# Attention and a gated layer on one core: all sums of GpSimd given to VectorE, and one order for all instructions drawn up anew

## The chip, the cores and the metric

The kernel runs on 1 core of one Trainium2 chip. The metric is device time in microseconds (us), the median of several runs; lower is better. The engines are TensorE (PE in the profile; its weight loads PEld), VectorE (DVE), ScalarE (ACT), GpSimd (POOL) and SyncE (SP), whose queue issues all transfers of this kernel.

## The reference

For each of 8 batches and 8 heads there are 512 tokens `x` (64 wide) and 32 states. Tokens attend to states and states to tokens; the two results, laid side by side as 8 x 544 rows of 512, go through a layer with a product of two branches.

```
a  = softmax(scale * x @ state.T);  xread = a @ state
a2 = softmax(scale * state @ x.T);  sread = a2 @ x
rows = concatenate([xread, sread], axis=2)      # 8*544 rows of 512
out  = ((rows @ w_a) * (rows @ w_b)) @ w_out    # 512 -> 1536 -> 512
```

## The kernel before

**The arithmetic.** Every large product is made of three matmuls, since each float32 operand is held as a high part (`_h`) and a remainder (`_l`): high by high, high by remainder, remainder by high. A high part is made by a ScalarE copy that rounds, its remainder by a VectorE subtraction: `g_h` and `g_l` of the gated value, `p_h` and `p_l` of the first weights, `at_h` and `at_l` of the attention, `ws_h` and `ws_l` of sums of weights. The weights of the first layer are folded with the states (`products`, or `project` by way of the DRAM tensors `scr`, read back as `p_raw`).

**The stages.** The 1536 inner columns are 12 tiles, two to a chunk `c` (0 to 5). `VISITS` walks the batches 0 to 3 over their chunks: `layer1` fills two PSUM tiles `ab` per inner tile, ScalarE copies the one into `a_sb`, VectorE multiplies the other with it, and `layer2` accumulates four `acc` tiles. Batches 4 to 7 come in pairs (`ROUNDS`, two rounds a pair): `make` lets `layer1` keep its product of 512 columns in `kept_g`, and seven calls of `term` multiply sums of the two batches' values with sums of the weights, seven block products in place of eight. Beside the rounds stand `attend` (attention of batches 4 to 7), `reading` (the states' side; it loads `a` from `e_dram` and `xn`) and the states' own layer (`states1`, `states2`, tiles `sw_st`).

**The sums that GpSimd makes.** They all go through `pool_op` (L1106). `combine(c)` (L1109) makes the sums of weights of a chunk: 2 of 512 columns into `wf` (high part and remainder joined), 4 of 256 columns into `ws`, and 2 remainders of 512 columns into `ws_l`, 8 in all; their results go to DRAM as `s_dram` and come back as `wt`. `term` (L1192) with k = 3 makes 4 sums of 512 columns: `kept_g` less `kept_g`, `t2w`, `kept_g` less `t2w`, and `kept_g` less `kept_g`. There are 6 chunks with 8 and 12 terms with 4, so 96 sums: 72 of 512 columns and 24 of 256.

**The order.** The program is first recorded, not issued: `Recorder` keeps each instruction (or a group that stays together) as a numbered unit in the order of the source. `ORDER` is a table of all unit numbers; `arranged` reads it, and the units are issued in that order, under `manual_schedule`. So the table alone sets the order of each engine's queue, of SP's too, and the order in which tiles take their turn in the pools (`ring` with 39 places, `lane` with 21, eight PSUM places). All instructions of a queue start in that order; one that waits holds those behind it.

Almost every instruction is issued at L1279 of the kernel before (L1286 of the changed one), so rows are told apart by their tiles' names.

Of the kernel before, what the change touches and what calls it, by code (L numbers as in the profile page):

```python
# [147 lines left out]
118 173 202-203 133 195 145 119 191 213 120 192 198 134 366 215 199 121 548 216 146 122 196 2571 217 135 200 220 136
152 370 224 153 219 147 536 137 204 138 221 154-155 193 148 231 149-150 534 201 374 151 236 223 537 2572 535 158 225
156 237 157 174 239 159 175 378 176 230 177 546 238 178-179 160 180 232 181 197 182 541 183 233 184 257 240 186  # L150
260-261 226 258 161 185 301 205 187 367 227 241 302 234 247 382 228 263 304 242 368 235 243 538 372 244 266 369 264
188 267 389 245 303 371 268 246 542 376 259 1001 248 373 249 253 250-251 189 375 252 294 539 265 291 262 254 540 288
269-270 377 255 271-272 305 379 273 285-286 543 380 547 810 275 2574 289 381 276 290 277 256 1010 278 274 1019 384 279
281 280 2577 2575 2578 396 383 282 385 283 325 287 397 306 284 326 399 307 391 308 386 309 398 310-312 400 318 295 313
387 390 314 322 334 1002 388 335 327 315-317 323 319 549 544 324 545 350 550 351 583 352 296 566 353 773 340 354 551
1006 355 392 336 341 555 567-568 337-338 292 320 342 552 343 1011 344-345 2676 553 331-332 339 569 293 346 328 1012
329 571 330 556 417 333 401 347 557 402-403 1028 1013 404 348 405 358 321 393 359 356 554 407 357 408 406 394 1020 360
409-410 1014 361 395 411 1007 412-413 420 457 2679 2677 558 414 1021 429 349 458 430-431 1015 559 432-433 460 435 2680
560 436 459 421 437 461 434 422 441 438 1016 439 362-364 440 365 448 442 418 415 462-463 561 464 416 465-467 1030 423
474 570 584 562 574 419 1004 563 424 443 425 1022 426-427 564 428 1005 468 585 490 565 469 1017 451-452 586 1018 453  # L160
484 445 587 1023 446 572 449 1008 450 470 588 573 454 481 455 575 447 1046 1009 482 1047 471 1025 485 1024 486 1062
1048 1037 472 1049 514 774 473 1029 491 475 492 775 493 1026 483 576 1063 444 510 476 511 1094 478 1027 456 477
487-488 496 577 497 578 498 494 499 579 1052 495 1050 479 489 512 1051 515 513 516 502 518 1064 500 580 501 524 589
503 590 1053 480 1039 504 651 581 595 652 596-597 654 591 653 592 506 655 507 593-594 1031 598 601 599 508 505 1038
600 519 602 617-619 517 620 712 1040 509 520 713 621 521 623 715 624-625 714 523 626-627 716 605-606 628 608 622 609
629 610 637 603 611 638-639 614 640 612 776 630 607 656-657 779 658 633-634 604 659-661 780 662 668 663 777 664-665
613 793 666 631 667 635 794 778 795 615 782 616 645 636 684 798 685-686 669 687-688 646 632 647 641 1032 642 690 783
691-692 781 693 784 643 672 649 648 689 785 675 297 694 644 696 695 1065 811 2682 697 298 525 786 812 1101 676 2685
1095 2683 678 813 679 717 814 2686 723-724 670 815 725 718-719 671 681 720-721 787 1041 722 726 729 727 673 728 878
730 1033 788 1042 789 680 745 751 1034 752 682 796 753 1035 677 754 1036 797 755 746 698 747 790 748 683 749 1043 791  # L170
756 750 1096 879 706-707 792 709 881 674 880 700 1044 701-702 1045 882 733-734 801 710 799 711 1054 1097 800 1056 1055
699 703 1057 704-705 736 1067 1058 1066 708 1059-1060 522 757 742 1068 739-740 1061 758 741 767 731 1069 768 1103 743
1102 1169 737 732 1070 1178 759 802 744 1072 1071 803 769 804 1073 1086 816 805 735 761 1087 762 817 806 1196 822 770
1187 738 807 763 823 1076 808 764 1104 818 1074 824 1075 819 765 1077 820 825 766 1105 1089 771 826 1088 1106 821 827
1108 828 772 760 939 1107 829 1098-1099 835 830 844 850 1100 1170 851 1171 845 832 1172 833 846-847 831 848-849 1173
852 856 853-854 1175 1179 855 838 857 841 1174 842 836 1180 940 883 834 1181 942 839 884 1176 843 941 840 1253 868
1177 943 869-870 858 872 1182 873 1188-1189 885-886 1184 887-888 1078 895 860 1079-1080 861 1090 1081 862 889 863 911
1091 912-913 1183 890-891 1185 892 1260 874 1186 837 893 871 894 864 896 1082 1084 859 1083 865 897 917 1190 866 918
867 1205 1085 899 914 900 1093 915-916 1092 901 923 1207 876 1197 919-921 1206 922 944 1208 924 945 1221 902 875 927
1222 1198 946 1191 905 650 950 1199 1192 1211 908 1193 1254 1328 951 1209 1255 1194 947 898 948 1195 952 1200 909 1210  # L180
910 1256 936 1201 949 1223 1202 928-929 1212 906 1262 1213 956 1224 903 1214 904 953 1257 937-938 969 1109 972 930 925
1229 1215 954 1216 907 955 1203 931 957 1337 1226 970-971 1261 1225 1233 1258 1204 997 960 1330 1259 1230 933 1263 978
934 958 1245 973 1110 932 1234 963 926 979 1329 980 998 974 1331 1217 975 1332 1218 1231 1334 1111 961 1227 976-977
1264 1247 1235 1232 962 964 1333 965 1246 935 1236 1219 984 966 981-982 1335 983 967 1336 985 968 994 1220 995 1265
996 1338 999 1228 1135 1339 1138 986 1346 959 1113-1114 1248 1237 1340 877 1139 1238-1239 1267 1341 1136 1266 1343
1342 1137 1163 1240 1164 1112 991 1364 1119 1365 1120 1140 1344 1241 1355 1249-1250 1380 1121 1345 1122-1123 1242 1124
1115-1118 1243 1125 988 1244 1368 1126 992 1347 1252 993 1348 1141 1369 1147 1349 1148 1132 1382 1133 1350 1366 1352
1351 1166 989 1149 987 1353 1142-1143 1127 990 1144 1129 1367 1128 1167 1145 1354 1381 1146 1357 1165 1251 1153 1370
1529 1134 1371 1150 1412 1151 1356 1152 1383 1160 1154 1372 1268 1168 1358 1373-1374 1297 1359 1375 1294 1130
1269-1270 1131 1385 1161 1361 1162 1360 2130 1291 1388 1271 1362 1390 1363 1295 1272 1414 1389 1278 1273 1391 1274  # L190
1404 1275 1155 1276 1384 1279 1376 1156-1157 1377-1378 1280 1386 1379 1277 1281 1284 1158 1387 1292 1282 1405 1283
1300 1419 1285 1293 1301 1426 1302 1298 1286 1531 1159 1396 2139 1303 1397 1304-1306 1312 1307-1308 1413 1288-1290
1487 1316 1415 1317 1488 1394 1416 1489-1490 1319 1318 1447 1417 1392 1491 1493 1421 1320 1393 1321 1418 1492 1309
2132 1395 1310 1296 1322 1420 1494 1323 1311 1407 2131 1402 1495-1496 1313 1406 1299 1325 1287 1448 1314 1326-1327
1422 1427 1456 1449 1429 2133 1457-1458 1606 1532 1400 1428 1450 1497 1484 2148 1430-1431 1401 1499 1432 1498 1315
1437 1433 1485 2134 1434 2140 1438 2136 2135 1500 1451 1501 1452 1439 2141 2137 1475 1324 2142 1502 2138 1476
1440-1441 2143 1435 1442 1503 1453 1436 1398 1504 1443 1454 1534 1455 1444 1481 2157 1459 1399 1509 1460 1510 1533
# [1124 lines left out]
```

## Time and profile before

| | |
|---|---|
| median of 3 runs | 695.41 us (694.81 to 695.91) |
| the profiled execution, its own time | 694.02 us |
| its span in the profile | 692.2 us |
| mean granted TensorE clock | 0.989 |
| PE busy | 654.6 us, 95% of the span |
| DVE busy | 543.5 us, 79% |
| ACT busy | 406.8 us, 59% |
| POOL busy | 132.6 us, 19%, 102 instructions |
| DMA | 164.26 MB, mean 237 GB/s |

The span runs from the program's first instruction to its last on the core. Busy time of an engine is the time in which at least one of its instructions ran; records of VectorE that follow each other overlap a little, so means of groups add up to more than the busy time. A released wait names who ended it.

### The profile page before, as it was taken

How to read it: one execution, taken by the hardware profiler on the slowest of the kernel's cores; microseconds unless marked ns; L12 is line 12 of the kernel's file. 1: busy time of each engine (PE TensorE's matmuls, PEld its weight loads, DVE VectorE, ACT ScalarE, POOL GpSimd, SP SyncE). 2: the span in 40 equal slices, each digit the busy share in tenths (PEclk: the TensorE clock that was granted, in tenths of full speed). 3: DMA queues.
4: the chain of work that ended last, by engine and by line, in shares of the span. 5: the costliest groups of instructions: out<-in, count | busy, mean ns of one | idle time of the engine just before them, and what ended most of it. 6: DMA issues, size and time to landing. Idle time of an engine off the chain costs nothing.

```text
span 692.2 us, 10431 instructions
## 1 busy us (share of the span) xinstructions
PE 654.6 (95%) x3624; PEld 514.0 (74%) x3624; DVE 543.5 (79%) x926; ACT 406.8 (59%) x760; POOL 132.6 (19%) x102
## 2 busy tenths in 40 slices
PE   7999999999998999998988899997999989998996
PEld 4777777878887787876766678776788868886885
DVE  6999978766658957769695695987898886678895
ACT  5796854789877857755443554452655536454452
POOL 0000000000227402282002430134001540025200
PEclk9999999999999999999999999999999999999999
DMA  9985254578898992996787971797844975595306
GB/s 333 356 299 199 75 183 177 184 293 305 301 342 316 320 300 90 324 308 196 258 251 243 332 279 41 240 324 226 354 154 118 321 292 169 184 331 198 121 1 152
DMA packets 123091, 164.26 MB, mean 237 GB/s; under 512 B 47008, under 2 KB 79776, under 8 KB 123040
## 3 DMA queue, kind: packets, MB, share of 16 engines
q1 hardware_dynamic: 123040, 163.61, 70.1%
q8 instruction: 28, 0.46, 0.3%
q14 instruction: 23, 0.19, 0.1%
HBM read 113.77 MB, written 49.81 MB: 236 GB/s over the span
## 4 chain that ended last, share of the span: by engine, by line
PE 65%; DVE 15%; DMA 7%; issue 5%; ACT 3%; SPq 2%; POOL 1%; DVEq 0%; ACTq 0%; POOLq 0%
PE ab L1279 30%; PE acc L1279 26%; PE ms L1279 9%; DMA p_raw<-scr 3%; DVE t L1279 3%; DVE g_l L1279 2%; SPq L1279 2%; DVE p_l L1279 2%; DVE stg L1279 1%; DMA xn<-xn 1%; DMA raw<-wl 1%; DMA wo_dram<-wo 1%; DVE kept_g L1279 1%; DVE turned L1279 1%; DVE m L1279 1%
## 5 line engine op out<-in xcount | busy, mean ns | idle before, releaser
L1279 PE MATMUL ab<-at_h,p_h 128*128 128x512 f32 x384 | 152.2, 403 | 20.3 <-DVE kept_g L1279 7.9
L1279 PE MATMUL ab<-at_l,p_h 128*128 128x512 f32 x384 | 150.7, 395 | 0.0
L1279 PE MATMUL ab<-at_h,p_l 128*128 128x512 f32 x384 | 149.9, 394 | 0.0
L1279 ACT COPY a_sb<-ab 128x512 f32<-128x512 f32 (+1 forms) x120 | 67.7, 565 | 120.4 <-PE ab L1279 117.9
L1279 PE MATMUL acc<-g_h,wo 128*128 128x512 f32 x384 | 126.5, 392 | 2.6 <-DVE stg L1279 2.6
L1279 PEld LDWEIGHTS ab<-at_h,p_h 128*128 128x128 f32 x384 | 72.5, 190 | 47.6 <-DVE kept_g L1279 10.5
L1279 PE MATMUL acc<-g_h,wt 128*128 128x512 f32 x336 | 105.9, 396 | 0.0
L1279 PEld LDWEIGHTS acc<-g_h,wo 128*128 128x128 f32 x384 | 71.8, 188 | 20.6 <-DVE stg L1279 3.5
L1279 PEld LDWEIGHTS ab<-at_l,p_h 128*128 128x128 f32 x384 | 73.2, 191 | 16.0 <-issue 1.3
L1279 PEld LDWEIGHTS ab<-at_h,p_l 128*128 128x128 f32 x384 | 73.1, 190 | 15.7
L1279 POOL TENSOR_TENSOR kept_g<-kept_g 128x512 f32<-128x512 f32 x24 | 36.1, 1503 | 249.4 <-DVE g_l L1279 98.8
L1279 PEld LDWEIGHTS acc<-g_h,wt 128*128 128x128 f32 x336 | 63.2, 190 | 15.2 <-issue 1.7
L1279 PE MATMUL acc<-g_l,wo 128*128 128x512 f32 x192 | 72.8, 393 | 0.0
L1279 DVE TENSOR_TENSOR a_sb<-ab,a_sb 128x512 f32<-128x512 f32 (+1 forms) x60 | 37.8, 631 | 43.2 <-PE ab L1279 21.5
L1279 PE MATMUL acc<-g_l,wt 128*128 128x512 f32 x168 | 66.0, 393 | 0.0
L1279 DVE TENSOR_TENSOR p_l<-p_raw,p_h 128x512 fp32r<-128x512 f32 x72 | 52.9, 762 | 11.7 <-ACT p_h L1279 11.7
L1279 POOL TENSOR_TENSOR wf<-wo 128x512 f32<-128x512 f32 x12 | 19.2, 1614 | 221.3 <-DMA raw<-wl 185.1
L1279 DVE TENSOR_TENSOR kept_g<-ab,a_sb 128x512 f32<-128x512 f32 x48 | 32.8, 683 | 31.7 <-PE ab L1279 23.8
L1279 DVE TENSOR_TENSOR g_l<-kept_g,g_h 128x512 fp32r<-128x512 f32 x72 | 54.0, 766 | 2.3 <-ACT g_h L1279 2.3
L1279 DVE SCALAR_TENSOR_TENSOR t<-t,t 128x512 int32<-128x512 int32 x60 | 47.7, 802 | 9.3 <-ACT t L1279 7.8
L1279 ACT CAST p_h<-p_raw 128x512 fp32r<-128x512 f32 x72 | 41.9, 620 | 18.4 <-DMA p_raw<-scr 18.3
L1279 ACT ACTIVATE t<-raw 128x512 f32<-128x512 f32 x72 | 48.1, 676 | 5.4 <-DMA raw<-wl 4.2
...
## 6 DMA issues: line engine op xcount, KB each, us to landing
...
```

Of the source, the lines that this page charges most:

```text
L1279: getattr(obj, method)(*map(real, args), **{k: real(x) for k, x in kw.items()})
```

## The change

`pool_op` now calls VectorE. The table `ORDER` is another one throughout (203 lines in place of 196): the units, their number and their work are the same.

```
-5 1 10 0 11 6 19 23 123 34-36 124 139 3 2 526 62 4 1003 37 48 38 7-8 527 39 9 49 21 40 50 12 206 20 69 582 22 24 51
+5 1 10-11 3 6 19 23 123 34-36 140 0 37 2 38-39 48 7 4 49 124 40 8 62 20 41 9 42 21 50 12 51-52 13 25 24 22 53 26-27 54
...
     def pool_op(out, in0, in1, op):
-        nc.gpsimd.tensor_tensor(out=out, in0=in0, in1=in1, op=op)
+        nc.vector.tensor_tensor(out=out, in0=in0, in1=in1, op=op)
```

What moves is seen on the engines' queues. Three places follow; a number at the end of a tile's name is the buffer's.

**The sums of weights.** Before, they stand on POOL, in six blocks, the first of them:

```order
L1279 TENSOR_TENSOR wf<-wo 128x512 x2
L1279 TENSOR_TENSOR ws<-wf 128x256
L1279 TENSOR_TENSOR ws<-ws,wf 128x256
L1279 TENSOR_TENSOR ws_l<-ws,ws_h 128x512
L1279 TENSOR_TENSOR ws<-wf 128x256
L1279 TENSOR_TENSOR ws<-wf,ws 128x256
```

Now they stand on VectorE, strewn among other work; of the first of them:

```order
L1286 TENSOR_TENSOR a_sb_1737<-ab_1722,a_sb_1737 128x512
L1286 TENSOR_TENSOR ws_1746<-wf_1133,ws_1759 128x256
L1286 TENSOR_SCALAR t2_1796<-raw_1401 128x512
L1286 TENSOR_TENSOR wo_1480<-t2_1188,wo_1480 128x512
L1286 TENSOR_TENSOR wf_1809<-wo_955 128x512
L1286 TENSOR_TENSOR wq_1789<-t2_1573,raw_1335 128x512
L1286 TENSOR_TENSOR ws_l_1821<-ws_1746,ws_h_1813 128x512
L1286 TENSOR_TENSOR ws_1833<-wf_1659 128x256
L1286 TENSOR_TENSOR ws_1782<-ws_1782,wf_1659 128x256
```

Between a sum (`ws_1746`) and its remainder (`ws_l_1821`), which needs ScalarE's copy `ws_h_1813` of it, stand four rows of other work; the products `a_sb` that TensorE waits for now share this queue with the sums.

**The sums of kept values.** VectorE before, in the second round of the pair of batches 4 and 5, from one product `kept_g` to the next one of the same round that the trace shows late (`xst`, `at_l`: the attention and the reading beside it):

```order
L1279 TENSOR_TENSOR kept_g_4908<-ab_4970,a_sb_4974 128x512
L1279 STREAM_TRANSPOSE a_tr_5016<-s_p_4379 128x512
L1279 TENSOR_TENSOR g_l_5023<-kept_g_4515,g_h_4995 128x512
L1279 TENSOR_TENSOR stg_4254<-acc_4934,stg_4254 128x16x32
L1279 TENSOR_TENSOR stg_4262<-acc_4943,stg_4262 128x16x32
L1279 TENSOR_TENSOR g_l_5047<-kept_g_4591,g_h_5012 128x512
L1279 TENSOR_TENSOR at_l_5057<-a_tr_5003,at_h_5027 128x512
L1279 TENSOR_TENSOR p_l_5065<-p_raw_4821,p_h_5033 128x512
L1279 TENSOR_TENSOR at_l_5057<-a_tr_5016,at_h_5027 128x512
L1279 TENSOR_TENSOR kept_g_5082<-ab_5051,a_sb_5053 128x512
```

Now, in the same round, from one such product to the next:

```order
L1286 TENSOR_TENSOR kept_g_5121<-ab_5081,a_sb_5101 128x512
L1286 COPY xst_4207<-ms_4889 64x2x32
L1286 TENSOR_TENSOR kept_g_4781<-kept_g_4781 128x512
L1286 TENSOR_TENSOR at_l_5103<-a_tr_5022,at_h_4988 128x512
L1286 TENSOR_TENSOR stg_4373<-acc_4872,stg_4373 128x16x32
L1286 TENSOR_TENSOR kept_g_4651<-kept_g_5121,kept_g_4651 128x512
L1286 TENSOR_TENSOR g_l_5154<-t2w_5069,g_h_5110 128x512
L1286 TENSOR_TENSOR kept_g_5121<-ab_5127,a_sb_5135 128x512
```

Before, eight rows stood between the two products and none was a sum of `term`; now six stand there, two of which are sums that POOL made before (`kept_g_4781`, `kept_g_4651`).

**The loads for the states' side.** SP's queue before, around the second block of `xn` and `a`:

```order
L1279 DMA xn<-xn 128x1024 x4
L1279 DMA a_3863<-e_dram_0_879 32x4x128 x4
L1279 DMA out<-turned 32x16x64 x4
L1279 DMA a_3863<-e_dram_1_1061 32x4x128 x4
L1279 DMA a_3979<-e_dram_0_1339 32x4x128 x4
L1279 DMA a_3979<-e_dram_1_1502 32x4x128 x4
L1279 DMA wt<-wo_dram_1652 128x4x128
L1279 DMA p_raw<-scr_1_2215 128x1024
L1279 DMA wt<-wo_dram_1930 128x4x128
```

Now, of the same loads:

```order
L1286 DMA a_3026<-e_dram_1_1592 32x4x128 x2
L1286 DMA xn<-xn 128x1024
L1286 DMA a_2995<-e_dram_0_1057 32x4x128
L1286 DMA a_2995<-e_dram_1_1492 32x4x128
L1286 DMA p_raw<-scr_1_1604 128x1024
L1286 DMA a_3283<-e_dram_1_1606 32x4x128
L1286 DMA s_dram_3117<-ws_l 128x2x256
L1286 DMA a_3026<-e_dram_0_1012 32x4x128
L1286 DMA stg<-part_1_1563 128x1024
L1286 DMA a_2995<-e_dram_1_1492 32x4x128
L1286 DMA a_2877<-e_dram_1_1473 32x4x128
L1286 DMA scr_1_3062<-sw 128x512
```

The sixteen loads `a` of the block stood together, with only `out` stores among them; now such loads stand singly or in twos between transfers of other kinds.

## Rows read from the trace of the kernel before

**Rows 1.** The page, part 1: busy us (share of the span) and instructions.

```profile
PE 654.6 (95%) x3624; PEld 514.0 (74%) x3624; DVE 543.5 (79%) x926; ACT 406.8 (59%) x760; POOL 132.6 (19%) x102
```

**Rows 2.** Who ended TensorE's waits: us in total, times, longest.

```profile
PE ab L1279 <- DVE kept_g L1279: 7.9, 4, 5.0
PE ab L1279 <- DVE a_sb L1279: 7.2, 4, 2.8
PE ab L1279 <- ACT a_sb L1279: 6.9, 7, 1.8
PE ms L1279 <- DMA a<-e_dram: 2.9, 1, 2.9
PE acc L1279 <- DVE stg L1279: 2.6, 2, 2.2
```

**Rows 3.** Stretches: length, busy PE, PEld, DVE, ACT, POOL (instructions), PEclk, DMA share, GB/s.

```profile
420.00:440.00 20.00, 20.00 (x100) 15.63 (x99) 14.75 (x27) 10.61 (x21) 0.00 (x0) 1.00 0.45 150
204.90:216.90 12.00, 10.21 (x46) 7.89 (x44) 11.79 (x13) 7.86 (x15) 9.03 (x9) 1.00 1.01 374
221.20:233.20 12.00, 10.65 (x47) 8.04 (x45) 11.08 (x11) 8.79 (x17) 11.84 (x10) 1.00 0.91 323
289.60:301.60 12.00, 11.28 (x50) 9.01 (x48) 7.89 (x9) 7.03 (x13) 10.12 (x9) 1.00 1.04 384
307.20:319.20 12.00, 9.43 (x41) 7.17 (x39) 12.00 (x18) 7.27 (x15) 9.22 (x8) 1.00 0.69 245
386.40:398.40 12.00, 10.43 (x49) 8.27 (x48) 11.18 (x18) 7.73 (x17) 7.49 (x5) 1.00 1.03 372
459.40:471.40 12.00, 7.01 (x31) 5.02 (x29) 11.90 (x17) 4.59 (x8) 7.96 (x5) 1.00 0.75 265
551.70:563.70 12.00, 9.14 (x44) 7.12 (x42) 11.76 (x12) 5.72 (x11) 10.09 (x7) 1.00 1.03 415
623.30:635.30 12.00, 9.51 (x47) 7.63 (x45) 10.61 (x16) 7.12 (x14) 6.43 (x5) 1.00 0.50 183
```

**Rows 4.** The same view, stretches just after TensorE's four longest waits.

```profile
381.70:386.30 4.60, 4.60 (x43) 3.65 (x44) 0.26 (x1) 0.91 (x2) 0.00 (x0) 0.63 0.93 267
471.40:475.00 3.60, 3.60 (x9) 2.83 (x10) 2.92 (x4) 0.00 (x0) 1.65 (x1) 0.53 0.52 145
563.70:567.20 3.50, 3.50 (x9) 2.76 (x10) 3.50 (x7) 1.34 (x3) 0.00 (x0) 0.51 0.62 255
635.30:638.90 3.60, 3.60 (x9) 2.84 (x10) 2.59 (x4) 0.17 (x1) 1.04 (x1) 0.53 0.95 307
```

**Rows 5.** VectorE's groups from 420 to 440 us: out<-in, shapes, count | busy us, mean ns.

```profile
L1279 DVE TENSOR_TENSOR g_l<-kept_g,g_h 128x512 fp32r<-128x512 f32 x5 | 3.3, 678 | 1.7 <-ACT g_h L1279 1.7
L1279 DVE TENSOR_TENSOR stg<-acc,stg 128x512 f32<-128x512 f32 x2 | 1.3, 666 | 0.0
```

**Rows 6.** VectorE's groups from 460 to 472 us.

```profile
L1279 DVE TENSOR_TENSOR at_l<-a_tr,at_h 128x512 fp32r<-128x512 f32 x2 | 3.5, 1755 | 0.0
L1279 DVE TENSOR_TENSOR p_l<-p_raw,p_h 128x512 fp32r<-128x512 f32 x2 | 2.4, 1210 | 0.0
L1279 DVE TENSOR_TENSOR stg<-acc,stg 128x512 f32<-128x512 f32 x2 | 1.3, 677 | 0.0
```

**Rows 7.** VectorE's groups over the whole span (forms kept apart).

```profile
L1279 DVE TENSOR_TENSOR g_l<-kept_g,g_h 128x512 fp32r<-128x512 f32 x72 | 54.0, 766 | 2.3 <-ACT g_h L1279 2.3
L1279 DVE TENSOR_TENSOR p_l<-p_raw,p_h 128x512 fp32r<-128x512 f32 x72 | 52.9, 762 | 11.7 <-ACT p_h L1279 11.7
L1279 DVE SCALAR_TENSOR_TENSOR t<-t,t 128x512 int32<-128x512 int32 x60 | 47.7, 802 | 9.3 <-ACT t L1279 7.8
L1279 DVE TENSOR_SCALAR t<-raw 128x512 int32<-128x512 uint32 x72 | 41.0, 577 | 11.1 <-DMA raw<-wl 8.6 <-DMA raw<-w_out 1.7 <-DMA p_raw<-scr 0.8
```

**Rows 8.** VectorE's groups from 583 to 600 us, where POOL has no row.

```profile
L1279 DVE TENSOR_SCALAR t<-raw 128x512 int32<-128x512 uint32 x2 | 0.8, 420 | 0.0
```

**Rows 9.** SP's queue in order of time: start us, us in which the transfers were issued.

```profile
372.76 5.73 SPq L1279 DMA_DIRECT2D a<-e_dram  x12
```

More of the change, by code (lines that the diff above doesn't have):

```diff
@@ L148 @@
[L148 to L197, printed above, removed]
@@ new lines @@
+2659 2539 2447 2442 2545 2589 2458 1804 2459 2540 2443 2541 2570 2309 2542-2544 2590 2546 2304 2591 2732 2579
+2592-2593 2460 2444 2704 2595 2445 2762 2416 2596-2597 2594 2598 2461 2599-2601 2701 2608 2602 2609 2733 2573 2610
+2249 2700 2611 2614 2702 2612-2613 2615 2705 2616 2320 2839 2617 2620 2618 2698 2622 2706 2451 2619 2623-2626 2621
+2627 2006 3190 2628 2638 2634 2629 2786 2703 2728 2630-2631 2640 2436 2576 2632-2633 2841 2635 2675 2580 2647 2681
+2648 2734 2641 2920 2642 2767 2336 2763 2842 2643-2644 2857 2645 3242 2437 2646 2417 2649 2901 2653 2650-2652 2912
@@ new lines @@
+3085 2725 2707 3195 2708-2711 2726 2684 2687 2724 2581 3176 2999 2840 2654 2713-2714 2712 2764 2858 2715 3169
+2716-2717 2820 2421 2587 2678 2588 2862 2719 2718 2754 2583 2755 2688 2729 2745 3253 2720 2696 2756 2730 2337 2425
+2870 2418 2768 2757 2693 2727 2420 2419 2748 2735 2921 2913 2871 2749-2751 3086 2752-2753 2760 2758-2759 2586 2821
+2765 2784 2769 2692 2825 2761 2770-2771 2863 2582 2739 2772 2776 2826 2777 2689 2828 2695 2773 2766 2827 2585 2872
+2778 2002 2690 2423 2779 2740 2774 2691 2780 2860 2584 2781 2694 2775 2741 2787 2897 3087 2782 2834 2829 2783
@@ new lines @@
+2736-2737 2849 2843 2850 2844 2790 2971 2845 3069 2422 2898 2791 2742 2792 2875 2923 2738 2851 2980 2867 2835 2822
+2846-2847 2868 2864 2848 2452 2902 2823 2852 2836 2876 2865 2922 2961 2853-2854 2824 2855 2972 2830 2883 2866
+2884-2885 3323 2856 2889 2924 3192 2973 2890 2831 2869 2874 2880-2881 2886-2887 3187 2837 2882 2981 2891 2888 2832
+3033 2983 2873 2877 2900 2892 2908 2001 2893-2894 2909 2895-2896 2796 2931 2903 2878-2879 2932 3104 2939 3174 2925
+2904 3000 3184 2926 3177 2859 2940 2910 2933 2905 2927 2906 2914 3008 2911 2907 2928 3088 2000 2833 2934 2917 2788
@@ new lines @@
+3071 3130 3012 3020 3013 2970 3028 3021-3022 3014 2793 3171 2808 3074 3072 2794 3029 3023-3024 3017 3254 3075
+3030-3031 3076 3036 3073 3032 3090 3175 3018 3091-3092 3079 3128 3053 3082 3327 3105 3134 2812 3039 3054 3283 3096
+3093 3080 3097 3492 3245 3146 3401 3098-3099 3083-3084 3094 3219 3095 3137 3313 3349 3182 3081 3131 3147 3100 3037
+3102 2795 3135 3345 3101 3325 3106 3120-3121 3136 3103 3221 3122 3173 3181 3344 3107 3143 3149 3114 3342 3110 3150
+3305 3314 3123 3811 3124 3252 3115-3117 3267 3218 3118 3178 3132 3038 2813 3108 3384 3058 3148 3144 3109 3119 3125
@@ new lines @@
+3503 3488 3474 3433 3467 3490 3529 3489 3434 3614 3504 3875 3469 3530 3476 3505 3477 3540 3506 3491 3507-3508 3512
+3539 3728 3513-3515 3509 3541 3599 4074 3426 4175 3533 3510 3748 3511 3548 3520 3531 3516 3544 3574 3897 3534 3905
+3749 3551 3611 3063 3542 3517 3768 3535 3518 3532 3568 3654 3552 3519 3386 3731 3615 3545 3521 3523 3064 3652
+3553-3554 3569 3555-3557 3536 3558 3571 3601 3559-3560 4031 3612 3563 3561 3600 3562 3065 3720 3570 3564 3719 3572
+3616 3585 3066 3602 3586 3603 3810 3604-3605 3591 3721 3592 3729 3643 3587 3577 3522 3593 3588-3589 3576 3051 3594
@@ new lines @@
+3812 3590 3595 3644 3617 3578 3711 3596-3597 3958 3598 3606 3619 3676 3620 3579 3835 3573 3067 3621 3618 3622
+3627-3628 3581 3629 3524 3582-3583 3630 3525 3623-3624 3631 3645 3769 3625 3584 3856 3632 3580 3716 3646 3626 3633
+3713 3634 3678 3635 3052 3636 3717 4037 3068 3655 3669 3638 4033 3834 3647 3656 3661-3662 3859 3657 3663 3658 3712
+3659-3660 3747 3664 3637 3665 3526 3667 3648 3803 3649 3670 3677 3730 3666 3679-3680 3668 3696 3687 3775 3714 3702
+3681 3715 3697-3698 3960 3947 3777 3948 3699 3703 3718 3700 3704 3701 3725 3770 3722 3857 3913 3708 3726 3732 3705
@@ new lines @@
+3832 3858 3841 3829-3830 3838 3860 4034 3831 3861 3808 3833 3862 3915 3684 3908 3899 3767 3765 3863 3976 3842 4039
+3900 3864 3686 3847 3867 3865 3909 3800 3866 3839 3868-3870 3977 3873 3764 3805 3902 3840 3871 3981 3903 3872 3883
+3874 3884 3843 3848 3885 3889 3852 4016 4169 3890 3801 4020 3891 3766 4066 4040 4035 3853-3854 3886 3691 3978 3887
+3809 3892 3806 3893 3910 4171 3888 4075 3979 3849 3894 3855 3850 3895 3941 3896 3917-3918 3986 3901 3925 3754 4176
+3916 3919 4017 3926 3987 3851 3920 3904 3921 3927 3944 3922-3924 3928 3982-3983 3929 3953 4067 3933 3930 3949
@@ new lines @@
+4205 3755 4166 4206 4131 4159 4375 4162 4187 4241 4189 4356 4215 4348 4188 4197 4190 4096 4167 4191 4238 4492
+4192-4193 4296 4222 4194 4164 4168 4242 4165 4195 4199 4196 4239 4211 4223 4207 4240 4643 4198 4200 4224-4226 4469
+4227 4243 4228 4357 4249 4212 4245 4307 4229 4216 4250 4234 4409 4230 4376 4201 4231-4232 4217 4308 4213 4233 4257
+4314 4219 4258 4545 4251 4208 4235 4214 4263 4246 4551 4264 4766 4259 4387 4260 4247 4261-4262 4470 4265 4209 4266
+4339 4522 4419 4218 4277 4309 4269 4281 4267 4374 4301 4268 4210 4248 4438 4282 4642 4270 4220 4283 4273 4284 4302
@@ new lines @@
+4648 4580 4402 4336 4441 4403-4404 4380 4443 4341 4553 4405 4418 4467 4344 4444 4593 4422 4442 4554 4382 4427 4383
+4822 4415 4406 4337 4547 4423-4424 4445 4468 4446 4408 4447 4203 4448 4701 4497 4650 4451 4449 4428 4450 4425 4493
+4384 4345 4452-4453 4459 4489 3757 4494 4454 4471 4829 4455-4456 4581 4457-4458 4460 4495 4583 4555 4472 4533 4548
+4462 4537 4473 4429 4534 4430 4498 4795 4461 4490 4477 4342 4474 4478-4480 4475-4476 4426 4499 4496 4519 4483 4481
+4486 4539 4651 4500-4501 4420 4482 4538 4549 4585 4516 4520 4463 4502 4540 4535 4523 4584 4503-4504 4484 4550
@@ new lines @@
+4595 4639 4749 4609 4689 4627 4654 4633 4577 4634 4596 4610 4728 4578 4680 4757 4635 4686 4750 4797 4687 4702 4677
+4655 4640 4688 4663-4664 4690 4678 4713 4636 4790 4717-4718 4656 4665 4579 4691 4666 4714 4698 4791 4695 4824
+4657-4658 4792 4694 4681 4696 4830 4667 4697 4798 4699-4700 4668 4602 4708 4703 4659 4709 4704 4679 4715 4705 4719
+4670 4660 4729 4682 4767 4710 4716 4672 4807 4725 4825 4706 4726 4722 4727 4723-4724 4808 4707 4739 4711 4809 4751
+4810 4826 4730 4758 4669 4752 4759 4831 4827 4857 4731 4740 4732 4799 4753-4754 4741 4733 4671 4742 4755 4734 4760
@@ new lines @@
+4811 4743 4746 4737 4800 4756 4801-4804 4763 4673 4768 4832 4805 4761-4762 4806 4769 4815 4770 4674 4764 4833 4747
+4771 4765 4744 4812 4675 4772 4813 4778 4773 4814 4736 4858 4834 4816 4774 4817 4779 4835-4836 4745 4818 4837 4819
+4838 4780 4735 4738 4861 4839 4777 4781 4842 4820 4840-4841 4843-4844 4859 4845-4849 4782 4862 4784 4863 4775
+4850-4852 4868 4860 4821 4853-4854 4865 4855 4869 4856 4866 4870 4785 4867 4776 4786 4872 4878 4783 4873-4875 4879
+4884-4887 4880 4877 4881 4888 4882 4876 4883
```

273 lines of the change are left out of this document (130 added, 143 removed), and 15 rows, old and new, of the table ORDER.

## The prediction

> **What bounds the kernel now.** I read the page's busy times first: TensorE is busy for 654.6 of the 692.2 us of the span, VectorE for 543.5, GpSimd for 132.6 [rows 1]. So a change that leaves TensorE's matmuls as they are can win only TensorE's idle time, and what its clock loses. The view of waits says who ended that idle time. Apart from the start and the end of the program it has five lines: VectorE's products `kept_g` 7.9 us, its `a_sb` 7.2, ScalarE's `a_sb` 6.9, VectorE's `stg` 2.6 and the loads `a` 2.9, together 27.5 us [rows 2]. So VectorE ends most of it, though it has a fifth of the span free: not its load as a whole is the matter, but what stands in front of the one result that TensorE needs.
>
> Next I took the 12 us in front of TensorE's waits, stretch by stretch. In eight of them GpSimd is busy for 6.4 to 11.8 us of the 12, though only 19% of the span; TensorE is idle there for 12 less its busy time, 1.79, 1.35, 0.72, 2.57, 1.57, 4.99, 2.86 and 2.49 us, in all 18.3 of the 27.5 us [rows 3]. From 420 to 440 us, with GpSimd idle, TensorE is busy throughout [rows 3].
>
> Why GpSimd's company is costly stands in VectorE's groups. With GpSimd idle a subtraction of 512 columns from SBUF takes 678 ns [rows 5]. From 460 to 472 us, with GpSimd at work, two of the same size take 1755 ns each and two others 1210 on the mean, while `stg`, one of whose inputs is in PSUM, takes 677 against 666 [rows 5, 6]. So it is neither VectorE as a whole nor the transfers that slow it: instructions that read SBUF alone are held while a sum runs on GpSimd. The Trainium skill says so of the hardware ("SBUF — State Buffer", section "SBUF: two separate sides"): the two engines share a pair of ports by an exclusive lock, and whoever comes second waits for the other's whole instruction; the trace agrees, with 1755 against 678 ns.
>
> Two more facts. After each of the four longest waits the granted clock reads 0.63, 0.53, 0.51 and 0.53 for 4.6, 3.6, 3.5 and 3.6 us, that is mostly the lower level, 1.2 GHz; by length times what is missing this loses 1.7 us each, 6.8 in all [rows 4]. TensorE had been idle for 2.5 to 5.0 us before each. And the wait for `a` came when SP issued twelve such loads in a row, in 5.73 us, with TensorE waiting for the last of them [rows 2, 9].
>
> **The change, part by part.**
>
> *The sums leave GpSimd.* VectorE gets 72 of 512 columns and 24 of 256. The first at 0.678 us [rows 5] are 48.8 us. For the second no row is close: between half of it and the whole of it, 0.34 and 0.678, they are 8.1 to 16.3 us. I take the middle, so 61 us in all, from 57 to 65.
>
> *VectorE is no longer held.* Four groups show what that gives back, by their means over the span against those without GpSimd: `g_l` 72 times 766 less 678 ns is 6.3 us, `p_l` 72 times 762 less 678 is 6.0, `t<-t,t` 60 times 802 less 678 is 7.4, `t<-raw` 72 times 577 less 420 is 11.3 [rows 5, 7, 8]: 31 us. Smaller groups add to it, so VectorE gains at most 61 less 31, 30 us, and ends at no more than 574 us busy, 86% of some 670. What hides these 30 us is the fifth of the span in which it is idle; if the sums stood where it is full, each would cost TensorE up to its 0.68 us. In the second place of the change's order two of them stand between two products `kept_g`, and the queue there is shorter than before all the same, six rows for eight.
>
> *What this is worth to TensorE.* Only one wait can be recomputed from rows: 4.99 us up to 471.4. In front of the product it waited for stood `at_l` twice and `p_l` once, at about 1.75 us each by the row of `at_l` [rows 6]; at 0.678 they take 3 x 1.08 = 3.2 us less, so some two thirds of that wait goes by the price alone. The lower bound for all eight is nothing, if other work becomes late in its place, and the upper one 18.3 us. Since the queues are also drawn up anew around the true prices, I take three quarters, **13.7 us**, nearest to the recomputed wait.
>
> *The clock.* Three of the four low stretches follow waits of this kind (4.99, 2.86, 2.49 us). The span's mean clock of 0.989 leaves 7.6 us below full speed, so these four, 6.8 us, are nearly all there is, and shorter waits have cost next to nothing of this kind. With the waits cut to a quarter, 3 x 1.7 = **5.1 us** come back.
>
> *The loads `a`.* They now stand singly or in twos between others, in place of sixteen in a block, so the last no longer stands behind eleven of its kind: the 2.9 us wait goes, and with it its own low stretch of 1.7, **4.6 us**. At worst another load comes late instead and nothing is won.
>
> *The remaining waits*, 27.5 - 18.3 - 2.9 = 6.3 us, have no GpSimd beside them. The new order redraws them too; I leave them as they are, between none and twice as much.
>
> *A wait that is added.* A remainder `ws_l` needs ScalarE's `ws_h`, and on VectorE it would hold `a_sb` behind it, and so TensorE. In the order shown four rows stand between the sum and its remainder, some 2 us of VectorE's work, and I cost it at nothing; without that cover it is one ScalarE copy each, 12 times. Sums of kept values wait for products of the same queue ahead of them, so for nobody new.
>
> *Sum*: 13.7 + 5.1 + 4.6 = 23.4, so the span becomes 692.2 - 23.4 = 668.8 us. The profiled execution's own time was 1.8 us over its span, and the median of the runs is 1.4 above that execution: 668.8 + 1.8 + 1.4 = **672.0 us**.
>
> **The rivals.**
>
> *VectorE becomes the bound* (slower). It holds that the sums add their full 61 us and nothing is given back. In the eight stretches GpSimd is busy for 72.2 us, VectorE idle for 7.8 [rows 3]. The sums of those stretches, 72.2/132.6 of 61 us, are 33.2 us; less 7.8 idle, TensorE would wait 25.4 us more: 692.2 + 25.4 + 3.2 = 720.8. It decides from the point at which the sums of those stretches, less what is given back there, are more than the 7.8 us that are idle. For it: VectorE is the busiest engine behind TensorE. The Trainium skill's "Perfetto Trace Analysis" speaks for it too: it has one relieve the engine of the highest occupancy first (section "Identifying the Most-Contended Engine"), and here that engine is given work. Against it: the rows of 1755 and 677 ns side by side, and sums spread far wider than on GpSimd. By that rule the time would be this rival's. Chance 0.04.
>
> *Transfers come late* (slower). The new queue of SP mixes loads and stores of all stages; a store that waits for its source holds the loads behind it. One late load at TensorE costs what the load of `a` cost, 2.9 and 1.7, 4.6 us [rows 2, 4]. It decides from six such waits, 27.6 us against the 23.4 won. Seven to nine would give 692.2 - 23.4 + 37 = 706 us, 709 as a median. For it: DMA shares of 1.01 to 1.04 in four of the eight stretches [rows 3], so transfers have little to spare. Against it: of the waits before only one was TensorE's for a load. Chance 0.06.
>
> *Half of it*: the long waits go, but the fuller queue of VectorE makes new short ones. Half of 23.4 is 11.7: 680.5 and 3.2, 683.7 us. Chance 0.24.
>
> *All of it*: the 27.5 us of waits and the 6.8 of the clock go, and span 657.9 gives 661.1. Chance 0.16.
>
> *The change does nothing* would need sums left on GpSimd or the old order; neither is the case, since no sum is left in GpSimd's queue. No change by way of gains and losses that cancel: 0.02.
>
> **How the numbers follow.** My forecast, 666 to 678 us around 672.0, has 0.48; with the half and the whole it makes 0.88 for faster by over 0.2% (1.4 us, about what a measurement of this kernel can tell from no change). Same 0.02, slower 0.10. The range runs from 657, just below the case in which all is won, to 692, well past the half, since the price of the new waits is bounded from one side only; the slower cases are left out, and they hold one in ten.
>
> **What would show it.** Right: VectorE's `g_l`, `p_l` and `t` near 680 ns with no mean above 700; VectorE's busy time between 540 and 575 us; TensorE's waits ended by VectorE at a few us in all; at most one low stretch of the clock in mid-run. Wrong: VectorE's busy time near 600 us and waits for `kept_g` and `a_sb` as long as now (first rival), or TensorE and ScalarE waiting for `p_raw`, `wt`, `raw` or `a` in many places, with low clocks behind them (second). If VectorE is freed and TensorE still waits for it, the new order, not the price, was misjudged.

## The result and the profile after

The changed kernel took 675.73 us (median of 4 runs, 673.59 to 676.49) where the kernel before took 695.11 (4 runs, 694.05 to 695.91): the ratio is 0.9717, with a 95% interval of 0.9691 to 0.9744. The forecast was 672.0. The profiled execution took 676.11 us, with a span of 674.3.

The page's busy times after, in answer to [rows 1]:

```profile
PE 653.7 (97%) x3624; PEld 509.8 (76%) x3624; DVE 540.4 (80%) x1022; ACT 407.1 (60%) x760; POOL 0.7 (0%) x6
```

VectorE runs 96 instructions more and is busy 3.1 us *less* than before. Why stands in its groups over the whole span, the answer to [rows 7], with three of the eight groups of sums that it took over beneath:

```profile
L1286 DVE TENSOR_TENSOR g_l<-kept_g,g_h 128x512 fp32r<-128x512 f32 x72 | 48.6, 683 | 7.5 <-DMA e_dram<-a_tr 4.9 <-PE acc L1286 1.8 <-ACT g_h L1286 0.6
L1286 DVE TENSOR_TENSOR p_l<-p_raw,p_h 128x512 fp32r<-128x512 f32 x72 | 48.5, 681 | 2.8 <-PE ab L1286 2.7
L1286 DVE SCALAR_TENSOR_TENSOR t<-t,t 128x512 int32<-128x512 int32 x60 | 40.7, 683 | 3.0 <-ACT t L1286 2.9
...
L1286 DVE TENSOR_TENSOR kept_g<-kept_g 128x512 f32<-128x512 f32 x24 | 16.3, 684 | 0.1
L1286 DVE TENSOR_TENSOR ws_l<-ws,ws_h 128x512 fp32r<-128x512 f32 x12 | 8.3, 688 | 5.0 <-ACT ws_h L1286 4.9
...
L1286 DVE TENSOR_TENSOR ws<-wf 128x256 f32<-128x256 f32 x12 | 5.0, 419 | 0.0
```

Every group with two inputs of 512 columns is now at 675 to 691 ns, where `g_l`, `p_l` and `t` were at 762 to 802; the one exception, `sd_l`, four instructions early in the program, has 1092 and had 1111 before, with GpSimd idle both times. The eight groups of sums add up to 58.9 us (the five not shown have three times 8.1 and twice 2.5).

What GpSimd's company had cost is found by adding up the durations of VectorE's instructions other than these sums: they were 600.5 us before and are 549.0 now. So the same work was held for **51.5 us**, 0.54 for each of the 96 sums, against 0.61 that a sum itself lasts on VectorE. That alone would leave a few us more than before. But durations of neighbours overlap, and the busy time counts an overlap once: in the program of its own below, 24 subtractions of 690 ns in a row keep VectorE busy for 14.5 us, 0.60 each. With 96 instructions more there is more overlap (608.1 us of durations in 540.4 busy, where it was 600.5 in 543.5). So what VectorE got back is about as much as what it was given, and its load did not grow.

Who ended TensorE's waits, in answer to [rows 2] (us in total, times, longest):

```profile
PE ab L1286 <- ACT a_sb L1286: 3.5, 3, 2.9
PE ab L1286 <- DVE kept_g L1286: 2.2, 2, 2.0
PE acc L1286 <- DMA wt<-wo_dram: 2.0, 1, 2.0
...
PE ms L1286 <- ACT wq L1286: 0.8, 1, 0.8
...
PE acc L1286 <- DVE g_l L1286: 0.7, 2, 0.5
...
PE ab L1286 <- DVE a_sb L1286: 0.3, 1, 0.3
```

With one more row of 0.3 (ScalarE's `sw`) these make 9.8 us in mid-run, where 27.5 stood; the rows left out belong to the start of the program. VectorE's `a_sb` fell from 7.2 to 0.3, `kept_g` from 7.9 to 2.2; `stg` and the loads `a` are gone. Three waits of two or three us are left, and they lie close together. TensorE's instructions of this stretch, in order of time, that waited for 2 us or more (in brackets the wait and its releaser), and under them one of VectorE and one of ScalarE from the same stretch:

```profile
438.58 0.47 PE L1286 MATMUL acc<-g_h,wt 128*128 128x512 f32 x1 [2.00 <-DMA wt<-wo_dram]
...
454.63 0.50 PE L1286 MATMUL ab<-at_h,p_h 128*128 128x512 f32 x1 [2.05 <-DVE kept_g L1286]
...
464.93 0.50 PE L1286 MATMUL ab<-at_h,p_h 128*128 128x512 f32 x1 [2.94 <-ACT a_sb L1286]
...
451.55 0.69 DVE L1286 TENSOR_TENSOR g_l<-kept_g,g_h 128x512 fp32r<-128x512 f32 x1 [4.91 <-DMA e_dram<-a_tr]
...
463.21 0.67 ACT L1286 ACTIVATE t<-raw 128x512 f32<-128x512 f32 x1 [5.97 <-DMA raw<-wl]
```

VectorE and ScalarE were idle there themselves, for 4.91 and 5.97 us, and both were released by transfers. SP's queue shows where these stood (start, us in which they were issued):

```profile
441.97 1.00 SPq L1286 DMA_DIRECT2D e_dram<-a_tr  x2
452.13 0.32 SPq L1286 DMA_DIRECT2D a<-e_dram  x1
452.54 0.38 SPq L1286 DMA_DIRECT2D wt<-s_dram  x1
...
455.88 0.36 SPq L1286 DMA_DIRECT2D raw<-wl  x1
```

```profile
SPq L1286 <- DMA e_dram<-a_tr: 9.1, 1, 9.1
```

Two stores `e_dram<-a_tr` are issued from 441.97 on, and the next entry is a load `a<-e_dram`. The second row, from the view of SP's own waits (440 to 470 us), says what it stood for: 9.1 us until a store `e_dram<-a_tr` had landed. For 9.2 us SP issues nothing, with `wt`, `raw` and `p_raw` behind. The windows view (as [rows 3]) of that stretch, and of stretches after the start and after the last two of these waits, with the granted clock behind POOL's column:

```profile
442.00:448.00 6.00, 6.00 (x130) 5.13 (x120) 4.26 (x11) 4.00 (x10) 0.00 (x0) 1.00 1.01 354
448.00:454.00 6.00, 4.58 (x22) 3.47 (x20) 2.45 (x7) 1.79 (x4) 0.00 (x0) 1.00 0.22 75
...
14.00:18.50 4.50, 4.42 (x29) 1.67 (x30) 4.43 (x11) 1.73 (x5) 0.00 (x0) 0.63 1.02 417
455.00:459.00 4.00, 4.00 (x12) 3.13 (x11) 3.69 (x9) 1.62 (x3) 0.00 (x0) 0.57 0.83 249
465.00:469.00 4.00, 4.00 (x33) 2.83 (x37) 0.44 (x1) 2.47 (x5) 0.00 (x0) 0.60 0.95 298
```

From 448 to 454 us the DMA engines have a share of 0.22: nothing had been given to them. After the last two waits, 2.05 and 2.94 us long, the clock reads 0.57 and 0.60 over 4 us, in answer to [rows 4], that is 1.2 GHz for most of it; a third low stretch, 0.63, follows the waits of the start and was not there before.

### The profile page after: what moved, and what is told of

The parts are those of the page before. It is cut to its first block, busy times and chain, and to the rows that moved or that the text cites. A ratio compares the mean times of both kernels' runs of the same rounds, so it can differ in the third digit from the quotient of the medians.

```text
span 674.3 us, 10321 instructions
## 1 busy us (share of the span) xinstructions
PE 653.7 (97%) x3624; PEld 509.8 (76%) x3624; DVE 540.4 (80%) x1022; ACT 407.1 (60%) x760; POOL 0.7 (0%) x6
## 4 chain that ended last, share of the span: by engine, by line
PE 57%; DVE 6%; DMA 2%; issue 1%; ACT 1%; SPq 0%; DVEq 0%; ACTq 0%
PE ab L1286 29%; PE acc L1286 22%; PE ms L1286 5%; DMA e_dram<-a_tr 1%; DVE kept_g L1286 1%; DVE turned L1286 1%; DVE g_l L1286 1%; DVE xst L1286 1%; DVE a_sb L1286 0%; SPq L1286 0%; DVE t L1286 0%; DVE stg L1286 0%; DMA a<-e_dram 0%; ACT g_h L1286 0%; ACT a_sb L1286 0%
## 5 line engine op out<-in xcount | busy, mean ns | idle before, releaser
L1286 PE MATMUL ab<-at_l,p_h 128*128 128x512 f32 x384 | 147.4, 393 | 0.0
L1286 PE MATMUL ab<-at_h,p_l 128*128 128x512 f32 x384 | 146.3, 393 | 0.0
L1286 PE MATMUL acc<-g_h,wo 128*128 128x512 f32 x384 | 133.4, 392 | 0.1
L1286 PE MATMUL acc<-g_h,wt 128*128 128x512 f32 x336 | 119.1, 395 | 2.0 <-DMA wt<-wo_dram 2.0
L1286 DVE TENSOR_TENSOR g_l<-kept_g,g_h 128x512 fp32r<-128x512 f32 x72 | 48.6, 683 | 7.5 <-DMA e_dram<-a_tr 4.9
L1286 PE MATMUL ab<-xs,sw_st 128*128 128x512 f32 (+1 forms) x192 | 51.1, 339 | 0.2 <-DVE kept_g L1286 0.2
L1286 DVE TENSOR_TENSOR p_l<-p_raw,p_h 128x512 fp32r<-128x512 f32 x72 | 48.5, 681 | 2.8 <-PE ab L1286 2.7
L1286 ACT COPY sw<-ms 128x512 f32<-128x512 f32 x72 | 41.4, 585 | 14.5 <-PE ms L1286 12.3
L1286 ACT CAST g_h<-kept_g 128x512 fp32r<-128x512 f32 x72 | 43.3, 621 | 11.2 <-DVE kept_g L1286 6.0
L1286 DVE TENSOR_TENSOR stg<-acc,stg 128x512 f32<-128x512 f32 x60 | 40.6, 685 | 9.7 <-PE acc L1286 9.4
```

What stands on the lines that cost most here:

```text
L1286: getattr(obj, method)(*map(real, args), **{k: real(x) for k, x in kw.items()})
```

## The experiments

**The engine alone, and the order alone.** The first takes the kernel before and changes one word; the second takes the changed kernel and puts that word back.

```diff
 # e1: the order of before;  e2: the new order, with the + and - exchanged
     def pool_op(out, in0, in1, op):
-        nc.gpsimd.tensor_tensor(out=out, in0=in0, in1=in1, op=op)
+        nc.vector.tensor_tensor(out=out, in0=in0, in1=in1, op=op)
```

> The old order with the 96 sums on VectorE, nothing else. Theory 1, the price (a sum on GpSimd holds VectorE's instructions that read SBUF, so taking GpSimd away is what wins): VectorE's groups of 512 columns all at 675 to 695 ns, VectorE busy 535 to 550 us, TensorE's waits in mid-run down from 27.5 to 10 to 16 us, the 2.9 us wait for the loads of a still there, time 675 to 684 us. Theory 2, the order (the sums moved ahead and the spread loads are what wins): time within 692 to 697. Theory 3, VectorE's load (96 more instructions are paid for in full): over 700.

Measured: 683.21 us (681.91 to 684.84), ratio 0.983 with an interval of 0.9798 to 0.9863. VectorE is busy for 543.4 us, within 0.1 of before. Its group `g_l`, and then the five largest rows of TensorE's waits:

```profile
L1279 DVE TENSOR_TENSOR g_l<-kept_g,g_h 128x512 fp32r<-128x512 f32 x72 | 48.0, 682 | 1.8 <-ACT g_h L1279 1.7
```

```profile
PE ab L1279 <- ACT a_sb L1279: 6.5, 8, 1.5
PE ab L1279 <- DVE kept_g L1279: 4.0, 5, 1.0
PE ms L1279 <- DMA a<-e_dram: 2.9, 1, 2.9
PE acc L1279 <- DMA wt<-s_dram: 1.9, 1, 1.9
PE acc L1279 <- DVE stg L1279: 1.7, 1, 1.7
```

The stretch with the longest wait of before tells it best. From 460 to 472 us, the kernel before and then this one:

```profile
460.00:472.00 12.00, 7.01 (x29) 5.04 (x28) 11.93 (x16) 4.59 (x8) 8.54 (x6) 0.98 0.75 265
```

```profile
460.00:472.00 12.00, 10.40 (x44) 7.83 (x44) 11.90 (x20) 4.47 (x8) 0.00 (x0) 1.00 0.75 249
```

VectorE is full in both, with the sums among its own work in the second. In the same 12 us it gets 20 instructions done instead of 16, and TensorE 10.40 us of work instead of 7.01. Theory 3, the load, falls. Taking GpSimd's company away, with the order left as it was, is worth 12.5 us (against 695.66 for the kernel before, run beside these two) of the 19.4. The mid-run waits, 18.9 us by these five rows and two of 1.1 and 0.8, are more than theory 1 expected.

TensorE's matmuls stand in the same order in these two kernels, so each wait can be looked up again. The eight waits beside GpSimd had 18.3 us before; at the same matmuls 5.2 are left (0, 0, 0.71, 1.70, 0.49, 1.54, 0 and 0.73). The longest, 4.99 us, is now:

```profile
466.70 0.50 PE L1279 MATMUL ab<-at_h,p_h 128*128 128x512 f32 x1 [1.54 <-ACT a_sb L1279]
```

So the price takes 13.1 us off these eight; the total falls by 8.6 only, since between 5 and 6 us of waits are new or longer at other places (1.9 of them for `wt<-s_dram`).

GpSimd could also have delayed TensorE by the lateness of its results. ScalarE did wait for its sums `t2w`, in the kernel before:

```profile
ACT g_h L1279 <- POOL t2w L1279: 19.2, 9, 7.6
```

But the two longest of these nine, 7.60 and 5.26 us, end at 476.8 and 402.7 us, behind TensorE's waits near them (up to 471.4 and 398.4) and not in front. And with the sums on VectorE in the same order ScalarE still waits 12.8 us for `t2w`, while the eight waits are down to 5.2. So this is not the main cause; that it has no part is not shown.

> The new order with the 96 sums on GpSimd, nothing else. Theory 1, the price: VectorE's means back at 750 to 810 ns, VectorE busy 520 to 545 us although it has 96 instructions fewer, TensorE's waits 20 us or more, time 690 to 705, so no gain over the kernel before. Theory 2, the order: 674 to 682. Theory 3, the load: below 675.7, since VectorE is freed of 59 us.

Measured: 688.69 us (684.62 to 692.26), ratio 0.9899 with an interval of 0.9874 to 0.9924. VectorE is busy for 536.1 us. Its durations add up to 595.1 us against the 549.0 of the same work in the changed kernel, so GpSimd's company costs it 46.1 us here, and its means are back up (`g_l` at 747 ns, `p_l` at 785):

```profile
L1286 DVE TENSOR_TENSOR p_l<-p_raw,p_h 128x512 fp32r<-128x512 f32 x72 | 55.9, 785 | 3.7 <-PE ab L1286 3.2 <-ACT p_h L1286 0.4
```

Both theories missed. Theory 1 had the order worth nothing without the price, and it is worth 7.0 us; theory 2 had it worth nearly everything. The two parts add: 12.5 + 7.0 = 19.5 us, against 695.11 - 675.73 = 19.4 for both together, as far as intervals of some 2 us either way can tell. Of the order's part the rows place the loads `a`: with the old order (e1) the 2.9 us wait and a clock of 0.51 over 3.5 us behind it are still there, with the new order there is no such wait, with or without GpSimd. The 7.0 us are what is left after a loss: the longest wait here, 4.97 us for ScalarE's `a_sb` up to 471.8 us, comes of the same load behind the same store as in the changed kernel. ScalarE was idle for 6.71 us until `raw` came, and SP had stood still (440 to 475 us):

```profile
SPq L1286 <- DMA e_dram<-a_tr: 7.9, 1, 7.9
```

So this hole belongs to the new order and not to the sums on VectorE.

**Which sums.** In two kernels with the new order only the sums of weights, or only those of kept values, go back to GpSimd.

```diff
+    def pool_op2(out, in0, in1, op):
+        nc.gpsimd.tensor_tensor(out=out, in0=in0, in1=in1, op=op)
 # e3: pool_op2 for the calls in combine;  e4: for those in term
```

> The changed kernel with only the 48 sums of weights (wf, ws, ws_l) back on GpSimd. Theory 1: in the four stretches where these sums stood before, TensorE waited 1.79, 1.35, 0.72 and 2.57 us, 6.4 in all, of which most comes back: 679 to 684 us. Theory 2: 674 to 678, as the order is the new one. Theory 3: 672 to 675.

> The changed kernel with only the 48 sums of kept values (kept_g, t2w) back on GpSimd. Theory 1: the four stretches with these sums had 1.57, 4.99, 2.86 and 2.49 us, 11.9 in all, and three low stretches of the clock of 1.7 each, so more comes back than with the weights: 684 to 693 us. Theory 2: 674 to 678. Theory 3: 672 to 675.

Measured: 679.30 us (ratio 0.9764, 0.9733 to 0.9794) and 686.28 (0.9871, 0.9835 to 0.9907), both as theory 1 had it. Against the changed kernel the weights cost 3.6 us and the values 10.6; the first interval just overlaps with that of the changed kernel, so its 3.6 us are not quite clear of noise, and the second is far off. Busy times of the two pages:

```profile
PE 653.4 (96%) x3624; PEld 508.5 (75%) x3624; DVE 535.7 (79%) x974; ACT 407.1 (60%) x760; POOL 56.7 (8%) x54
```

```profile
PE 659.6 (96%) x3624; PEld 511.1 (74%) x3624; DVE 540.0 (79%) x974; ACT 406.8 (59%) x760; POOL 75.0 (11%) x54
```

The durations of VectorE's instructions, without the sums left to it, add up to 566.8 and 576.4 us, against 549.0 in the changed kernel: 48 sums of weights hold VectorE for 17.9 us, 48 sums of values for 27.4. A sum of values holds it for 0.57 us, about the 0.60 for which one in a row keeps it busy when VectorE makes it; a sum of weights, some of them half as long, for 0.37.

**The price by itself.** A program of its own: stages of 24 VectorE instructions, alone and beside GpSimd's, on tiles that have nothing to do with each other.

```python
STAGES = [  # name, VectorE's instruction, GpSimd's
    ("v_ss", "ss", None), ("v_ss_p_ss", "ss", "ss"), ("v_ss_p_s", "ss", "s"), ("v_ss_p_set", "ss", "set"),
    ("v_ps_p_ss", "ps", "ss"), ("v_s", "s", None), ("v_s_p_ss", "s", "ss"), ("v_s_p_s", "s", "s"), ("v_s_p_set", "s", "set"),
    ("v_r", "r", None), ("v_r_p_ss", "r", "ss"), ("p_ss", None, "ss"), ("p_s", None, "s"), ("p_set", None, "set"),
]   # ss: two inputs in SBUF; ps: one in PSUM; s: one input; r: the form of t<-raw; set: memset
```

> A program of its own, that computes nothing of the reference: 24 VectorE instructions of 512 columns per stage, alone and beside GpSimd instructions of 512 columns that need nothing from them. Theory 1, a lock on what reads SBUF: VectorE's two-input subtraction 670 to 690 ns alone, 1200 ns or more on the mean beside GpSimd's two-input subtraction; with one input in PSUM 670 to 700 beside the same; the one-input form of t<-raw 420 alone and 900 or more beside it; beside GpSimd's memset, which reads nothing, no more than 700. Rival, that any work of GpSimd takes VectorE's time: beside memset also over 900, and with one input in PSUM too.

VectorE's groups (the first part of a name is VectorE's instruction, the second what GpSimd did; busy us, mean ns):

```profile
L48 DVE TENSOR_TENSOR v_ss_p_ss_v<-a,b 128x512 f32<-128x512 f32 x24 | 27.3, 1212 | 0.0
L54 DVE TENSOR_SCALAR v_r_p_ss_v<-raw 128x512 int32<-128x512 uint32 x24 | 20.8, 945 | 0.0
L52 DVE TENSOR_SCALAR v_s_p_ss_v<-a 128x512 f32<-128x512 f32 x24 | 20.8, 944 | 0.0
...
L52 DVE TENSOR_SCALAR v_s_p_set_v<-a 128x512 f32<-128x512 f32 x24 | 19.1, 878 | 0.0
...
L48 DVE TENSOR_TENSOR v_ss_p_set_v<-a,b 128x512 f32<-128x512 f32 x24 | 14.5, 688 | 0.0
L48 DVE TENSOR_TENSOR v_ss_v<-a,b 128x512 f32<-128x512 f32 x24 | 14.5, 690 | 0.0
L50 DVE TENSOR_TENSOR v_ps_p_ss_v<-acc,b 128x512 f32<-128x512 f32 x24 | 14.4, 688 | 0.0
...
L52 DVE TENSOR_SCALAR v_s_v<-a 128x512 f32<-128x512 f32 x24 | 8.1, 424 | 0.0
L54 DVE TENSOR_SCALAR v_r_v<-raw 128x512 int32<-128x512 uint32 x24 | 8.1, 426 | 0.0
```

Theory 1 holds in each number that it gave. Twelve GpSimd sums make 24 subtractions last 27.3 us instead of 14.5: **1.07 us of VectorE for each sum on GpSimd**, where a sum on VectorE itself takes 14.5 / 24 = 0.60. (In the kernel a sum on GpSimd cost 0.54 on the mean. VectorE is not always at work there, part of its work reads PSUM, and a quarter of the sums are half as long; how much each of these makes is not shown.) For the form of `t<-raw` it is (20.8 - 8.1) / 12 = 1.06. With one input in PSUM it takes 688 beside GpSimd's sums; this form was not run alone, but in the kernel `stg`, which has one input in PSUM, took 681 with GpSimd at work and 685 without. Two inputs beside a memset lose nothing either (688). The rival falls for these, but not for every form: one input in SBUF beside memset takes 878 instead of 424.

**The queue of SP.** What is left at 430 to 470 us was tried in four versions of the changed kernel, by moving DMA issues in the order (a unit, and the one that it is put behind; shown for all four together):

```diff
+MOVES = [(3060, 3059), (3044, 3043),    # e6: two stores behind their transposes
+         (3357, 3607), (3354, 3565), (3355, 3354), (3352, 3355),    # and four loads of it later
+         (3218, 3219),                  # e7: also a half of wt behind its other half
+         (3345, 3356), (3344, 3345), (3342, 3344),    # e8: also three loads a later
+         (3811, 3810)]                  # e9: also a load wt to its other half
 def arranged(units):
...
+    for u, v in MOVES:
+        order.remove(u)
+        order.insert(order.index(v) + 1, u)
```

> The changed kernel with six DMA issues of SP moved, 429 to 463 us: two stores e_dram<-a_tr directly behind the transposes that make them, four loads of what they store behind other loads. Theory, the queue (a load that waits for a store's landing held SP from 443 to 452 us, and with it raw, wt and p_raw; two waits of TensorE, 2.05 and 2.94 us, and two low stretches of the clock of 1.7 came of it): 667 to 671 us, DMA at work from 446 to 452 us, the 2.0 us wait for wt at 438 still there. Rival, the transfers' rate (the stretch has more to move than the DMA engines can): the same waits for raw and a_sb a little later, 673 to 677.

Measured: 670.47 us (670.16 to 670.91), ratio 0.963 with an interval of 0.9602 to 0.9657, wholly below that of the changed kernel: 5.3 us less. In SP's queue no hole of 9 us is left, `raw` is issued 6 us earlier, and from 448 to 454 us the DMA engines have a share of 1.05 instead of 0.22:

```profile
441.26 0.47 SPq L1292 DMA_DIRECT2D e_dram<-a_tr  x1
...
449.62 0.33 SPq L1292 DMA_DIRECT2D raw<-wl  x1
```

```profile
448.00:454.00 6.00, 5.80 (x28) 4.52 (x27) 3.72 (x9) 2.17 (x4) 0.00 (x0) 1.00 1.05 385
```

The waits of 2.05 and 2.94 us are down to 0.4 and 0.6, no low clock follows them, and the wait for `wt` stays, all as the theory had it. So the late transfers of the changed kernel were a matter of what stood in the queue in front of them.

> As the one before, and one half of a tile wt issued directly behind its other half, some 4 us earlier in SP's queue. Theory, the queue: the 2.0 us wait at 438 goes too, 664 to 669 us, waits in mid-run below 3 us in all and at most one low stretch of the clock, that at the start. Rival, the rate: no better than the one before.

Measured: 670.66 us (668.99 to 672.46): no better, so the theory's 664 to 669 was missed, and the rival's forecast of the time was met. The wait for `wt` is gone, but in the same place, at 438.9 us, TensorE now waits for the loads `a`, two waits in the stretch:

```profile
PE ms L1292 <- DMA a<-e_dram: 2.5, 2, 1.7
```

> The version with the stores and wt moved, and three more loads a moved behind twelve others: they stood behind the store of what they load, and SP was held by the first of them from 424.9 to 430.1 us, while from 430 to 436 the DMA engines had a share of only 0.36. Theory, the queue: the loads that TensorE waited for at 438.9 us (1.71) and 461.7 (0.81) are issued some 5 us earlier, both waits go, 2.5 us less than the 670.66 of the version before: 667 to 669. Rival, the rate: the waits for a move by less than 1 us, 670 to 671.5.

Measured: 669.56 us (668.39 to 670.16), ratio 0.9622 (0.9602 to 0.9643): not to be told from the two before. The waits for `a` are gone, and a new one of 2.28 us for `a_sb` ends at 449.8 us, some 9 us later than the first of them. The row of the waits, that of ScalarE's copy into `a_sb`, and SP's queue:

```profile
PE ab L1292 <- ACT a_sb L1292: 2.5, 2, 2.3
```

```profile
449.15 0.59 ACT L1292 COPY a_sb<-ab 128x512 f32<-128x512 f32 x1 [3.22 <-DMA e_dram<-a_tr]
```

```profile
430.64 0.95 SPq L1292 DMA_DIRECT2D a<-e_dram  x2
435.32 0.34 SPq L1292 DMA_DIRECT2D e_dram<-a_tr  x1
```

With three loads fewer in front, SP comes to the first moved store at 431.6 us and stands there until 435.3, as its source is not yet made: where SP stood for 5.2 us (424.9 to 430.1) it now stands for 3.7 a little later, with a store at the end. The new wait is put down to another store, issued at 441.0 us while the DMA engines were full. Whether it comes of the shifted hole is not shown. SP still stands at an issue that is not ready in these versions (5.4 us with the first edit, 5.2 with the second, 3.6 here), so the queue theory holds on that; what this edit would win, it had wrong.

> As the one before, and a load wt (256 KB) that stood some 650 places ahead of its first use is moved to its other half, away from the crowded stretch. Theory, the queue: no more than 0.5 us on either side of the version before. Rival, the rate: 0.7 us less for the bytes taken out of the stretch, or a new wait for this tile later on, up to 2 us more.

Measured: 670.23 us (667.39 to 671.33, ratio 0.9629, 0.9602 to 0.9656), neither theory set apart. Its four runs go with the granted clock: 667.39 us at 1.000, and 669.55 to 671.33 at 0.990 to 0.992. Steps of half a us are not to be had against that. The four versions all beat the changed kernel by 5 to 6 us, and which of them is the best stays open.

## Why the prediction was right, and where it was off

*VectorE is relieved by what it is charged*: right in the outcome, two sizes were off. I had counted 31 us of relief, from four groups, against 61 us of sums, and so +30 at most. The sums were 58.9 us (the 24 of 256 columns took 0.42, inside the bounds of 0.34 and 0.678). The four groups gave back 30.4, as forecast, but the groups that I left as "smaller groups add to it" gave 21 more, 51.5 us in all. And I added means of instructions to a busy time, which counts the overlap of neighbours once; that is why it fell by 3.1 where the durations rose by some 7. That the load would not decide followed from any of these numbers, and the kernel with the old order showed it: 12.5 us faster at the same busy time of VectorE.

*The waits with GpSimd beside them*: right, and by the mechanism. I took three quarters of 18.3, 13.7 us; at the same matmuls, with the old order, the price alone took 13.1. The one that I recomputed by the price, 3.2 of 4.99 us, lost 3.45. With 2.9 for the loads `a` I had 16.6 us, and 27.5 - 9.8 = 17.7 went. What I left out is that waits come new elsewhere: with the old order they brought the gain of the price down to 27.5 - 18.9 = 8.6, and with the new order the three of two or three us came. That 17.7 is so near to 16.6 is in part luck, since older waits outside the eight went too, which I had left standing.

*The clock*: this is the term that was mis-sized. I had 6.8 us (5.1 and 1.7) coming back; of the four low stretches two are left in mid-run and one is new at the start, so one stretch, 1.7 us, came back. My sign for being right, at most one low stretch in mid-run, was missed: both stand behind the new waits. 17.7 + 1.7 is 19.4 against the 17.9 us by which the span fell (692.2 to 674.3), and 1.5 us are not placed. So the span came out 5.5 us above the 668.8 of the sum: 5.1 too much for the clock, 1.5 not placed, less the 1.1 more that the waits gave. In the time the miss is 3.7 only, because this profiled execution lies 0.4 above its median, where I had added 1.4 for one that lay below; these 1.8 us are luck.

*The loads `a`*: right. There is no wait for them and no low clock behind it with the new order, and both are there with the old one.

*The remaining waits, 6.3 us*: about right in sum, by luck, and wrong in kind. They did not stay: nearly all of those left, 2.00, 2.05 and 2.94, are new, and come of transfers. This is the second rival, *transfers come late*, with its mechanism word for word ("a store that waits for its source holds the loads behind it"), save that here a load waits for a store. It came in one stretch with three waits, not in six. Two of them came of the one hole, and cost 5.3 us with the clock behind them, by the version that undoes it.

*The wait for `ws_h`*: costed at nothing, rightly for TensorE. VectorE does wait for it, 4.9 us in all by its row above, and none of TensorE's waits names `ws_l`.

The rival *VectorE becomes the bound* fell, and with it, here, the rule of the Trainium skill's "Perfetto Trace Analysis" (section "Identifying the Most-Contended Engine") that stands beside it, to optimize the engine of the highest occupancy first: in VectorE's occupancy 51.5 us of being held were counted as work. *Half of it* (683.7) happens to be the engine's move without the order (683.2), though not by its mechanism.

One thing stays open. The new order with GpSimd (e2) has some 9 us less of waits in mid-run than the kernel before, but the span of its profiled execution is shorter by 4.1 only; TensorE's busy time is 4.0 us longer there, with as many low stretches, and no row here says why.
